# Moving the small steps of LayerNorm's reciprocal root from VectorE to GpSimd in a four-layer attention kernel, with new scheduling limits

## The chip, the cores and the metric

The kernel runs on one core of a Trainium2 chip. The core has a matrix engine (TensorE, PE in the profile; PEld are its weight loads), a vector engine (VectorE, DVE), an engine for activation functions (ScalarE, ACT), a general engine (GpSimd, POOL) and one that here only issues transfers (SyncE, SP). Each executes its own instructions in order and waits for the others by semaphores. The metric is device time of one execution in microseconds; less is better.

## The reference

The input is 2048 tokens of 512 features in bf16. Four residual layers follow each other, of two kinds, A, B, A, B. Each takes the LayerNorm of the running sum (mean and variance over the 512 features, no scale or shift):

```python
def _layernorm(x, axis=-1, eps=1e-05):
    m = jnp.mean(x, axis=axis, keepdims=True)
    v = jnp.var(x, axis=axis, keepdims=True)
    return (x - m) / jnp.sqrt(v + eps)
```

Both kinds have 32 heads of 16 features. Layer B is full softmax attention over all 2048 tokens. Layer A works on four segments of 512 tokens: causal softmax attention inside a segment, mixed by a gate per head with a linear attention over a memory `M`, `z` that the segments before have filled through `phi(t) = where(t > 0, t + 1, exp(t))`. Both end in a projection with 512 x 512 weights, which is added to the running sum.

## The kernel before

A `Builder` writes the program out ahead of time. All instructions pass through a recorder (`Sched.add`), which keeps an order for each engine, derives the semaphore waits from buffers read and written, and keeps a running estimate of when each engine will be free. The builder's choices hang on this estimate and on limits; the dictionary `PLAN` gives limits for each stretch of 40 units, and `set_limits` (called in `attention`) puts them in force.

The main loop, `attention`, goes by units. A unit (`unit`) makes scores of two or three banks, each 128 keys by 512 queries of one head, on TensorE, and one ScalarE instruction turns them into exponentials, 128 x 1024 or 128 x 1536 (L1691, tile `pT`). The weighted sums with the values, whose 17th column counts the denominators, follow two units later. There are 1549 units. In a unit with two banks for ScalarE one or two more banks can go to VectorE, which makes exponentials out of integers: a first affine step reads the scores from PSUM (L1213), then two shifted copies of 1024 or 2048 columns follow (L1267, L1284), and TensorE adds the three.  Their tiles lie in `dxt` or in the spare room of `KA`, `QA`, `VA`, `wA` and `wB`. In layer A the causal mask is added by a matmul with `tri` or set by GpSimd on the exponentials (L1705). GpSimd also makes most masked copies of queries (L1581, `qm`) and multiplies in the division by the denominators (L1838, `ob`), where `POOL_DIV` is 1.

All else is background work, generators that yield what they need next and how much of TensorE and VectorE it takes: `task_A` and `task_B` (LayerNorm, transposes, projections of one segment), `task_mem`, `task_out`. After each unit `background` runs as much of it as the credits allow. PSUM copies go to VectorE, or to ScalarE where the estimate has VectorE later by `EVAC_ACT` (`evac`, L603 and L605). `keep_busy` and `fill_gap` (L560) put matmuls with zeros into holes of TensorE.

LayerNorm of a segment is `ln_part`: statistics of four tiles of 128 tokens on VectorE (L714, L716), then the reciprocal root of four variances for each of 128 tokens, on a tile `lnw` of 128 x 4. For the first segment ScalarE computes it (L722). For the 15 others eight small VectorE steps do it: the variance plus epsilon (L727), a first guess by integer arithmetic on the bits (L729), and two Newton steps of three instructions (L732 to L734). Then `normalize` (L743) writes the normalized tile `xn`, on VectorE, or on GpSimd in stretches with `POOL_XN=1`, and a transposing DMA (L612, on SP) brings it into `xT` for the projections. `xn` has two buffers, so the third tile waits for the first one's transfer.

Of the kernel before, what the change touches and what calls it, by code (L numbers as in the profile page):

```python
# [7 lines left out]
ALU = mybir.AluOpType  # L8
# [9 lines left out]
LN_EPS = 1e-5  # L18
# [310 lines left out]
class Builder:  # L329
# [3 lines left out]
        1: dict(ACT1=400, R_LATE=1200, DX_BANK=700, NEAR=18, FILL_DVE=400, BACK=3, CR_W=1900, CR_B=1800, R_PAIRS=2, PAIRS=24, DIV_LATE=800, DVE_LATE=800),  # L333
        2: dict(MARGIN=500, DX_BANK=900, NEAR=8, SLACK=550, EARLY=300, FILL=0.42, CR_B=1200, PART=3, NEARW=20, PAIRS=60, BUSY_WAIT=500, DX_FIN=3000, POOL_QM=1, POOL_XN=1),
        3: dict(ACT1=600, NEAR=8, TAKEN_A=1, SLACK=550, PV_SKIP=900, FILL_DVE=200, BACK=8, CR_W=1900, NEARW=20, OPART=2, TAKEN=0.4, LOW=14, DVE_LATE=800, QWAIT=8, HOLD_AT=40, PHI_LATE=0),
        4: dict(R_LATE=1200, NEARW=40, PAIRS=24, MASK_PE=800, LEVEL=3, TAKEN=0.5, LOW=30),
        5: dict(R_LATE=1500, DX_LATE=900, REST=12, NEAR=8, TAKEN_A=1, R_NEAR=50, PV_SKIP=500, FILL_DVE=400, BUSY_ROOM=900, CR_W=1300, DX_LAG=1, LOW=20, HOLD_SEGS=2),
        6: dict(ACT1=600, NEAR=10, PV_SKIP=200, DX_LAG=3, MASK_PE=800, LEVEL=3, DIV_LATE=2500, BG_BANK=100, QUAD=0),
        7: dict(ACT1=400, REST=16, NEAR=3, SLACK=350, R_NEAR=10, EARLY=0, FILL_DVE=200, BUSY_ROOM=300, CR_B=1800, R_PAIRS=2, PAIRS=999, TAKEN=0.3, QWAIT=8, QMIN=3, HOLD_AT=12, LN1_AT=6),
# [9 lines left out]
        17: dict(MARGIN=800, NEAR=5, SLACK=350, R_NEAR=10, PART=3, OPART=3, PAIRS=60, DIV_LATE=2500, TAKEN=0.4, DVE_LATE=800),
        18: dict(DX_LATE=900, DX_BANK=700, REST=20, PV_SKIP=100, BUSY_ROOM=900, FILL=0.57, CR_A=1700, PART=3, R_PAIRS=2, OPART=4, MASK_PE=800, DVE_LATE=800, BG_BANK=100, QUAD=0, QWAIT=3, QMIN=4),  # L350
        19: dict(MARGIN=600, R_LATE=1200, DX_LATE=900, PV_SKIP=500, FILL_DVE=100, BACK=6, CR_B=1200, R_PAIRS=2, MASK_PE=800, DIV_LATE=2500, BUSY_WAIT=500, QWAIT=3, QMIN=4),
        20: dict(MARGIN=600, DX_LATE=900, EVAC_ACT=300, SLACK=550, PV_SKIP=100, CR_B=1200, R_PAIRS=2, MASK_PE=800, DIV_LATE=2500, BUSY_WAIT=500, GAP=1, BG_BANK=100, QWAIT=3, QMIN=3, HOLD_AT=40, LN1_AT=6, BUSY_BACK=800),
        21: dict(FILL_DVE=200, BACK=10, FILL=0.53, CR_W=1300, CR_B=1800, CR_A=1700, CARRY_W=0, NEARW=20, LEVEL=3, BG_BANK=400, QMIN=1, HOLD_MAX=0),
        22: dict(ACT1=200, DX_LATE=500, NEAR=10, PV_SKIP=200, EARLY=500, FILL=0.53, CR_B=1800, CARRY_W=1500, OPART=2, DX_LAG=1, MASK_PE=800, LEVEL=3, DIV_LATE=800, DVE_LATE=800, BG_BANK=100, QUAD=0, LN1_AT=6),
        23: dict(R_LATE=1200, R_NEAR=50, FILL_DVE=200, BACK=8, CR_A=1200, NEARW=40, OPART=4, PAIRS=999, LEVEL=3, TAKEN=0.25, QUAD=0, QMIN=4, HOLD_SEGS=2),
        24: dict(R_LATE=1500, DX_LATE=900, EVAC_ACT=100, REST=12, NEAR=8, TAKEN_A=1, SLACK=250, R_NEAR=50, PV_SKIP=100, EARLY=500, FILL_DVE=200, CR_W=1300, CR_A=1200, DX_LAG=1, LOW=20, BG_BANK=100, POOL_QM=1),
        25: dict(ACT1=300, MARGIN=600, R_LATE=2200, EVAC_ACT=1500, NEAR=18, CR_W=1900, CR_B=1800, R_PAIRS=2, DX_LAG=1, PAIRS=999, DIV_LATE=800, TAKEN=0.5, DVE_LATE=800, BG_BANK=400, PHI_LATE=300),
        26: dict(MARGIN=500, DX_LATE=700, REST=10, SLACK=350, EARLY=500, FILL_DVE=200, BUSY_ROOM=300, BACK=8, CR_W=1500, R_PAIRS=2, PAIRS=24, DIV_LATE=800, TAKEN=0.3, BG_BANK=100, QWAIT=8, QMIN=4, LN1_AT=6),
        27: dict(MARGIN=800, DX_BANK=700, REST=4, NEAR=10, SLACK=350, EARLY=500, FILL_DVE=200, BUSY_ROOM=300, BACK=8, CR_W=1500, PART=1, R_PAIRS=2, PAIRS=24, TAKEN=0.3, BG_BANK=100, QWAIT=8, QMIN=4, LN1_AT=6),
        28: dict(EVAC_ACT=800, NEAR=5, SLACK=350, R_NEAR=10, BACK=6, CARRY_W=400, NEARW=40, OPART=3, PAIRS=60, DIV_LATE=2500, BUSY_WAIT=0, TAKEN=0.3, DVE_LATE=800, BUSY_BACK=800),  # L360
        29: dict(DX_BANK=900, SLACK=700, PV_SKIP=100, EARLY=100, FILL_DVE=200, BUSY_ROOM=300, BACK=10, FILL=0.47, CR_W=1500, PART=3, R_PAIRS=2, TAKEN=0.3, DVE_LATE=800, LN1_AT=3, BUSY_BACK=800),
        30: dict(ACT1=300, MARGIN=800, REST=12, SLACK=700, PV_SKIP=100, EARLY=100, BACK=6, FILL=0.42, CR_W=1500, CARRY_W=400, PART=3, R_PAIRS=2, MASK_PE=800, DIV_LATE=2500, DVE_LATE=800, QWAIT=3, HOLD_MAX=0),
        31: dict(DX_LATE=700, DX_BANK=700, REST=20, PV_SKIP=100, BUSY_ROOM=900, FILL=0.57, CR_A=1700, PART=3, R_PAIRS=2, OPART=4, DX_LAG=3, MASK_PE=800, BUSY_WAIT=500, TAKEN=0.3, DVE_LATE=800, BG_BANK=100, QMIN=4, DX_FIN=3000),
        32: dict(MARGIN=400, NEAR=12, PV_SKIP=100, FILL_DVE=100, BUSY_ROOM=300, FILL=0.55, CR_W=1500, CARRY_W=400, R_PAIRS=2, OPART=3, GAP=3, DVE_LATE=800, QWAIT=8, QMIN=1, HOLD_AT=40, POOL_QM=1),
# [3 lines left out]
        36: dict(ACT1=300, DX_LATE=900, DX_BANK=700, REST=20, NEAR=3, PV_SKIP=900, BUSY_ROOM=900, FILL=0.57, CR_B=1800, CR_A=1700, PART=3, R_PAIRS=2, NEARW=90, OPART=3, DX_LAG=1, MASK_PE=200, LOW=20, DVE_LATE=800, QWAIT=3, QMIN=4),
        37: dict(MARGIN=400, NEAR=12, PV_SKIP=100, FILL_DVE=100, BUSY_ROOM=300, FILL=0.55, CR_W=1500, CARRY_W=400, R_PAIRS=2, OPART=3, GAP=3, DVE_LATE=800, QMIN=1, HOLD_AT=40, POOL_QM=1),
        38: dict(DX_LATE=700, REST=8, SLACK=250, R_NEAR=20, CR_W=1300, R_PAIRS=2, NEARW=90, PAIRS=999, LEVEL=1, LOW=20, GAP=1, DVE_LATE=800, BG_BANK=400, QUAD=0),  # L370
# [3 lines left out]
    MASK_PE = 500  # L374
# [1718 lines left out]
```

## Time and profile before

| | |
|---|---|
| median of 3 runs | 1736.19 us (1736.08 to 1737.96) |
| profiled execution | 1740.29 us |
| its span, first to last instruction | 1738.5 us |
| granted TensorE clock, mean | 0.996 |
| instructions | 46910 |

The profile's page gives each engine's busy time and share of the span, then the chain of work that ended last, by engine and by line, then groups of instructions: line, engine, operation, tile written and tiles read, shapes and count, then busy time in us and mean duration in ns, then the idle time of the engine just before them with what ended it. Busy time of a group is a union: where instructions overlap, it is less than count times mean. A list of one tile's or line's instructions gives minimum, median and maximum in ns. A table by windows gives each engine's busy time and instruction count, the granted clock, the share of DMA and GB/s. In the timeline the first two columns are the start and the duration in us. A list of waits gives total time in us, how often, and the longest.

### The profile page before, as it was taken

Reading aid. Unit: us, or ns where it says so; the run is one execution under the profiler, and the core shown is the slowest. Engines: PE = TensorE matmul, PEld = TensorE weight load, DVE = VectorE, ACT = ScalarE, POOL = GpSimd, SP = SyncE. Lnnn points to the kernel's source line nnn. Section 1 sums busy time; section 2 is a strip of 40 time slices with the busy share of each in tenths; the row PEclk is TensorE's granted clock in tenths of the full one; section 3 lists DMA queues with packets and bytes.
Section 4 is the critical chain, followed back from the end, with each engine's and each line's share of the span. In section 5 each row is a group of like instructions: output and inputs, shape, how many; then the busy total and the mean of one; then the engine's idle time right before and its main releaser. Section 6 shows DMA issues by size and latency. Waiting matters only on the chain.

```text
span 1738.5 us, 46910 instructions
## 1 busy us (share of the span) xinstructions
PE 1623.1 (93%) x19531; PEld 577.5 (33%) x19531; DVE 1521.2 (88%) x2928; ACT 1700.7 (98%) x1595; POOL 211.8 (12%) x321
## 2 busy tenths in 40 slices
PE   8999899999999999999999999999999999999999
PEld 5553434322222523522225222432222222222226
DVE  6757576999998689899996999889999999999997
ACT  8899999999999999999999999999999999999998
POOL 3211301110200402100003010110011000000000
PEclk9999999999999999999999999999999999999999
DMA  6210211000202131102111211011011000000000
GB/s 177 38 20 19 38 20 26 14 14 7 35 20 59 32 93 32 33 10 56 47 22 30 47 41 44 8 31 39 8 26 38 10 14 14 19 11 17 16 14 18
DMA packets 148438, 54.56 MB, mean 31 GB/s; under 512 B 128768, under 2 KB 147712, under 8 KB 148224
## 3 DMA queue, kind: packets, MB, share of 16 engines
q1 hardware_dynamic: 148224, 51.56, 13.8%
q8 instruction: 153, 2.51, 0.6%
q14 instruction: 61, 0.50, 0.1%
HBM read 18.88 MB, written 2.10 MB: 12 GB/s over the span
## 4 chain that ended last, share of the span: by engine, by line
ACT 48%; PE 31%; issue 13%; DVE 7%; SPq 0%; POOL 0%; DMA 0%; ACTq 0%; DVEq 0%
ACT pT L1691 47%; PE ps L545 31%; DVE KA L1213 1%; DVE dxt L1213 1%; ACT amem L810 1%; DVE lnst L714 1%; SPq L612 0%; DVE wA L1213 0%; PE ps L560 0%; POOL xn L743 0%; DVE VA L605 0%; DVE qm L1581 0%; DVE dxt L1267 0%; DVE dxt L1284 0%; DVE VB L605 0%
## 5 line engine op out<-in xcount | busy, mean ns | idle before, releaser
L1691 ACT ACTIVATE pT<-ps 128x1024 bf16<-128x1024 f32 (+1 forms) x1549 | 1668.6, 1246 | 24.4 <-PE ps L545 19.8
L545 PE MATMUL ps<-qm,KB 32*128 32x512 bf16 x4096 | 559.7, 385 | 79.5 <-ACT pT L1691 64.3
L545 PE MATMUL ps<-pT,VB 128*17 128x512 bf16 x2909 | 494.7, 384 | 2.1 <-DVE KA L1213 0.5
L545 PEld LDWEIGHTS ps<-qm,KB 32*128 32x128 bf16 x4096 | 145.0, 91 | 606.5 <-ACT pT L1691 518.3
L1213 DVE TENSOR_SCALAR KA<-ps 128x512 uint16<-128x512 f32 (+1 forms) x413 | 295.2, 724 | 13.0 <-PE ps L545 8.7
L1213 DVE TENSOR_SCALAR dxt<-ps 128x512 uint16<-128x512 f32 (+1 forms) x325 | 232.6, 721 | 16.5 <-PE ps L545 13.3
L545 PE MATMUL ps<-dxt,VB 128*17 128x512 bf16 x993 | 217.6, 381 | 0.0
L545 PEld LDWEIGHTS ps<-pT,VB 128*17 128x17 bf16 x2909 | 115.6, 87 | 285.7 <-issue 271.3
L1838 POOL TENSOR_TENSOR ob<-tb,rd 128x512 bf16<-128x512 bf16 x31 | 33.9, 1092 | 801.9 <-DVE rd L1834 801.9
L1213 DVE TENSOR_SCALAR wA<-ps 128x512 uint16<-128x512 f32 (+1 forms) x169 | 120.8, 723 | 2.6 <-PE ps L545 1.2
L545 PE MATMUL ps<-QA,VB 128*17 128x512 bf16 x420 | 118.3, 384 | 0.0
L1705 POOL TENSOR_SCALAR_AFFINE_SELECT pT<-pT 128x256 bf16<-128x256 bf16 (+4 forms) x128 | 67.6, 541 | 413.8 <-ACT pT L1691 413.8
L545 PE MATMUL ps<-woB,zero 128*32 128x512 bf16 (+1 forms) x353 | 117.5, 382 | 0.1
L545 PE MATMUL ps<-VA,VB 128*17 128x512 bf16 x420 | 114.1, 382 | 0.0
L545 PE MATMUL ps<-wA,VB 128*17 128x512 bf16 x534 | 113.1, 381 | 0.0
L545 PE MATMUL ps<-qm,KA 32*128 32x128 bf16 (+2 forms) x1536 | 93.6, 256 | 17.8 <-ACT pT L1691 12.8
L1581 POOL TENSOR_SCALAR qm<-QB,par 128x512 bf16<-128x512 bf16 x98 | 79.5, 821 | 234.8 <-PE ps L545 215.8
L545 PE MATMUL ps<-VA,pT 128*128 128x51 bf16 (+1 forms) x2540 | 103.9, 187 | 2.1 <-POOL pT L1705 0.9
L545 PE MATMUL ps<-KA,VB 128*17 128x512 bf16 x420 | 101.0, 383 | 0.0
L545 PEld LDWEIGHTS ps<-VA,pT 128*128 128x128 bf16 x2540 | 89.6, 96 | 20.9 <-issue 7.3
L1267 DVE TENSOR_SCALAR dxt<-dxt 128x1024 uint16<-128x1024 uint16 (+1 forms) x216 | 85.7, 420 | 1.2
L1213 DVE TENSOR_SCALAR wB<-ps 128x512 uint16<-128x512 f32 (+1 forms) x108 | 84.6, 792 | 1.6 <-PE ps L545 1.0
(167 smaller groups left out, 1946.6 us busy)
## 6 DMA issues: line engine op xcount, KB each, us to landing
wB<-in_B_wqkv_dram SPq DMA_DIRECT2D x48, 128.0 KB, 2.3
wA<-in_A_wk_dram SPq DMA_DIRECT2D x16, 128.0 KB, 2.2
wA<-in_A_wq_dram SPq DMA_DIRECT2D x16, 128.0 KB, 2.3
wA<-in_A_wv_dram SPq DMA_DIRECT2D x16, 128.0 KB, 2.4
out_dram<-x SPq DMA_DIRECT2D x8, 256.0 KB, 2.2
x<-in_A_x_dram SPq DMA_DIRECT2D x3, 512.0 KB, 9.5
wB<-in_B_wqkv_dram SPq DMA_DIRECT2D x1, 1536.0 KB, 11.8
oT<-ob SPq DMA_TRANSPOSE x63, 2.4
```

The costliest lines, as they stand in the source:

```text
L545: self.sc.add("pe", lambda e: e.matmul(out, lhsT, rhs, start=start, stop=stop, skip_group_check=True), reads=reads, banks=[(bank, "w", all ...
L714: self.op("dve", (lambda i, t: lambda e: e.bn_stats(st[:, k, i, 0:6], self.x[:, t, :]))(i, t), reads=[self.b_x[t]], writes=[bs], ns=690, p ...
L810: self.op("act", lambda e: e.activation(et, src, ACT.Exp), reads=bsrc, writes=self.b_amem, ns=1023, gap=915)
L1213: self.op("dve", lambda e: e.tensor_scalar(d, o, SCALE * LOG2E * 128, 127.0 * 128 + EXP_BIAS, op0=ALU.mult, op1=ALU.add), writes=[self.b_d ...
L1267: self.op("dve", (lambda d, s, c: lambda e: e.tensor_scalar(d, s, float(c), None, op0=ALU.add))(d, s, c), reads=[self.b_dxt[b][0]], writes ...
L1581: self.op(eng, (lambda m, q, col: lambda e: e.tensor_scalar(m, q, col, 0.0, op0=ALU.mult, op1=ALU.add))(m, q, col), reads=[bq, self.b_par] ...
L1691: self.sc.add("act", (lambda dst, src: lambda e: e.activation(dst, src, ACT.Exp, scale=SCALE))(dst, src), writes=self.b_pT[slot * 3 + i:sl ...
L1705: self.op("pool", (lambda blk, pat: lambda e: e.affine_select(blk, blk, pattern=pat, compare_op=ALU.is_ge, fill=0.0, base=0, channel_multi ...
L1838: self.op(eng, lambda e: e.tensor_tensor(ob, t[:, :, :, 0:16], rb, ALU.mult), reads=[br] + self.b_tb, writes=self.b_ob[oi], **(dict(ns=125 ...
```

## The change

GpSimd adds epsilon to the variances and does both Newton steps; VectorE keeps the integer first guess between them. A Newton step `y * (1.5 - 0.5 * v * y * y)` was three instructions, two of them with a scalar and two tensors; it now is four, three plain products and one affine step `-0.5 * t + 1.5`. So nine instructions on GpSimd and one on VectorE take the place of eight on VectorE, for each of 15 segments. In the recorder such a step has `ns=125, gap=110`, and the background work no longer reserves 560 ns of VectorE's credit for a Newton step.

All stretches of `PLAN` but the first and the last get other limits; among them four with `POOL_DIV=0` (10, 15, 16, 25; none before), and `POOL_XN=1` in stretches 2, 13, 22 and 24 (2 and 13 before). With them the whole order after the first units is another one.

```diff
@@ Builder.PLAN
...
-        22: dict(ACT1=200, DX_LATE=500, NEAR=10, PV_SKIP=200, EARLY=500, FILL=0.53, CR_B=1800, CARRY_W=1500, OPART=2, DX_LAG=1, MASK_PE=800, LEVEL=3, DIV_LATE=800, DVE_LATE=800, BG_BANK=100, QUAD=0, LN1_AT=6),
+        22: dict(ACT1=200, DX_LATE=900, NEAR=10, PV_SKIP=200, EARLY=500, BACK=3, FILL=0.53, CR_B=1800, CARRY_W=1500, OPART=2, DX_LAG=1, MASK_PE=800, LEVEL=3, DIV_LATE=800, GAP=1, DVE_LATE=800, BG_BANK=100, QUAD=0, LN1_AT=6, POOL_XN=1),
...
-        24: dict(R_LATE=1500, DX_LATE=900, EVAC_ACT=100, REST=12, NEAR=8, TAKEN_A=1, SLACK=250, R_NEAR=50, PV_SKIP=100, EARLY=500, FILL_DVE=200, CR_W=1300, CR_A=1200, DX_LAG=1, LOW=20, BG_BANK=100, POOL_QM=1),
+        24: dict(R_LATE=1500, DX_LATE=900, EVAC_ACT=100, REST=12, NEAR=8, TAKEN_A=1, SLACK=250, R_NEAR=50, PV_SKIP=100, EARLY=500, FILL_DVE=200, CR_W=1300, CR_A=1200, CARRY_W=1500, DX_LAG=1, LOW=20, POOL_QM=1, POOL_XN=1),
...
+    POOL_LN = 1
...
@@ Builder.ln_part
-        self.op("dve", lambda e: e.tensor_scalar(v, var, LN_EPS, None, op0=ALU.add), reads=self.b_lnst[k], writes=[bw], ns=165)
+        root = "pool" if self.POOL_LN else "dve"
+        step = lambda fn, reads: self.op(root, fn, reads=reads, writes=[bw], **(dict(ns=125, gap=110) if self.POOL_LN else dict(ns=165)))
+        step(lambda e: e.tensor_scalar(v, var, LN_EPS, None, op0=ALU.add), self.b_lnst[k])
         vi, yi = v.bitcast(dt.int32), y.bitcast(dt.int32)
         self.op("dve", lambda e: e.tensor_scalar(yi, vi, -0.5, RSQRT_MAGIC, op0=ALU.mult, op1=ALU.add), reads=[bw], writes=[bw], ns=165)
         for it in range(2):
-            yield [], 0, 560
-            self.op("dve", lambda e: e.scalar_tensor_tensor(tt, y, -0.5, y, op0=ALU.mult, op1=ALU.mult), reads=[bw], writes=[bw], ns=165)
-            self.op("dve", lambda e: e.tensor_tensor(tt, tt, v, ALU.mult), reads=[bw], writes=[bw], ns=165)
-            self.op("dve", lambda e: e.scalar_tensor_tensor(y, tt, 1.5, y, op0=ALU.add, op1=ALU.mult), reads=[bw], writes=[bw], ns=165)
+            yield [], 0, 560 * (not self.POOL_LN)
+            step(lambda e: e.tensor_tensor(tt, y, y, ALU.mult), [bw])
+            step(lambda e: e.tensor_tensor(tt, tt, v, ALU.mult), [bw])
+            step(lambda e: e.tensor_scalar(tt, tt, -0.5, 1.5, op0=ALU.mult, op1=ALU.add), [bw])
+            step(lambda e: e.tensor_tensor(y, tt, y, ALU.mult), [bw])
         return k
```

More of the change, by code (lines that the diff above doesn't have):

```diff
@@ L336 @@
[L336 to L339, printed above, removed]
@@ L349 @@
[L349 to L352, printed above, removed]
@@ L368 @@
[L368 to L370 removed]
+        1: dict(ACT1=400, R_LATE=1200, DX_BANK=700, NEAR=18, TAKEN_A=1, FILL_DVE=400, BACK=3, CR_W=1900, CR_B=1800, R_PAIRS=2, NEARW=20, PAIRS=24, MASK_PE=800, DIV_LATE=800, DVE_LATE=800),
@@ new lines @@
+        2: dict(MARGIN=500, DX_BANK=900, NEAR=8, SLACK=550, EARLY=300, FILL=0.42, CR_B=1200, PART=3, NEARW=20, PAIRS=60, BUSY_WAIT=500, LOW=30, QMIN=1, PHI_LATE=300, DX_FIN=3000, POOL_QM=1, POOL_XN=1),
+        3: dict(ACT1=600, REST=4, NEAR=8, TAKEN_A=2, SLACK=550, PV_SKIP=900, FILL_DVE=200, BACK=8, CR_W=1900, NEARW=20, OPART=2, TAKEN=0.4, LOW=14, DVE_LATE=800, QWAIT=8, HOLD_AT=40, PHI_LATE=0),
+        4: dict(R_LATE=1200, DX_LATE=700, EVAC_ACT=1500, FILL=0.4, R_PAIRS=0, NEARW=40, PAIRS=24, MASK_PE=800, LEVEL=3, TAKEN=0.5, LOW=30),
@@ new lines @@
+        5: dict(R_LATE=1500, DX_LATE=900, REST=12, NEAR=8, TAKEN_A=1, R_NEAR=50, PV_SKIP=500, FILL_DVE=400, BUSY_ROOM=900, FILL=0.47, CR_W=1300, PART=1, DX_LAG=1, LOW=20, HOLD_SEGS=2),
+        6: dict(ACT1=600, NEAR=10, PV_SKIP=200, CARRY_W=0, DX_LAG=3, MASK_PE=800, LEVEL=3, DIV_LATE=2500, BG_BANK=100, QUAD=0),
+        7: dict(ACT1=400, REST=16, NEAR=3, SLACK=350, R_NEAR=10, EARLY=0, FILL_DVE=200, BUSY_ROOM=300, CR_B=1800, PART=1, R_PAIRS=2, OPART=2, PAIRS=999, TAKEN=0.3, QWAIT=8, QMIN=3, HOLD_AT=12, LN1_AT=6),
@@ new lines @@
+        8: dict(MARGIN=800, NEAR=10, BACK=2, CR_W=1300, NEARW=40, DX_LAG=1, DIV_LATE=2500, BUSY_WAIT=0, DVE_LATE=800, QWAIT=3, QMIN=3, HOLD_MAX=0, PHI_LATE=300),
+        9: dict(ACT1=400, DX_BANK=700, NEAR=18, SLACK=350, FILL_DVE=400, BACK=3, CR_W=1900, CR_B=1800, R_PAIRS=2, PAIRS=24, DIV_LATE=800, DVE_LATE=800),
+        10: dict(R_LATE=1000, DX_LATE=500, DX_BANK=700, NEAR=5, TAKEN_A=1, SLACK=350, R_NEAR=50, CARRY_W=0, R_PAIRS=2, PAIRS=999, DIV_LATE=800, BUSY_WAIT=0, TAKEN=0.5, PE_LOW=4, DVE_LATE=1700, BG_BANK=100, QUAD=0, HOLD_MAX=0, PHI_LATE=300, LN1_AT=6, POOL_DIV=0),
@@ new lines @@
+        11: dict(R_LATE=1200, DX_LATE=900, R_NEAR=10, EARLY=0, BUSY_ROOM=900, FILL=0.42, CR_A=1200, OPART=4, MASK_PE=800, DIV_LATE=2500, DVE_LATE=800, BG_BANK=400, QMIN=4, HOLD_SEGS=2, PHI_LATE=0, POOL_QM=1, BUSY_BACK=800),
+        12: dict(ACT1=300, MARGIN=600, R_LATE=2200, EVAC_ACT=1500, NEAR=18, CR_W=1900, CR_B=1800, R_PAIRS=2, DX_LAG=1, PAIRS=999, DIV_LATE=800, TAKEN=0.5, DVE_LATE=800, BG_BANK=400, PHI_LATE=300, DX_FIN=3000),
+        13: dict(MARGIN=350, R_LATE=1500, DX_LATE=900, TAKEN_A=1, EARLY=300, BUSY_ROOM=300, CARRY_W=1500, PART=3, OPART=3, PAIRS=999, MASK_PE=800, BUSY_WAIT=0, GAP=3, QUAD=0, QWAIT=3, HOLD_SEGS=2, POOL_XN=1),
@@ new lines @@
+        14: dict(ACT1=200, DX_LATE=500, PV_SKIP=200, CARRY_W=0, DX_LAG=3, LEVEL=3, DIV_LATE=2500, BG_BANK=100, QUAD=0),
+        15: dict(ACT1=400, MARGIN=400, R_LATE=2200, EVAC_ACT=300, DX_BANK=700, REST=8, TAKEN_A=2, PV_SKIP=500, EARLY=300, FILL_DVE=400, BUSY_ROOM=400, BACK=4, CR_W=2200, CR_A=1700, CARRY_W=400, PART=1, DX_LAG=3, DIV_LATE=800, DVE_LATE=800, BG_BANK=100, POOL_DIV=0),
+        16: dict(ACT1=200, DX_LATE=500, PV_SKIP=200, DX_LAG=3, MASK_PE=800, LEVEL=3, DIV_LATE=2500, BG_BANK=400, QUAD=0, POOL_DIV=0),
@@ new lines @@
+        17: dict(MARGIN=800, NEAR=5, SLACK=350, R_NEAR=10, BACK=3, PART=3, OPART=3, PAIRS=60, DIV_LATE=2500, TAKEN=0.4, BG_BANK=100, POOL_QM=1),
+        18: dict(ACT1=200, DX_LATE=500, NEAR=10, PV_SKIP=200, EARLY=500, FILL=0.53, CR_B=1800, OPART=2, DX_LAG=1, MASK_PE=800, LEVEL=3, DIV_LATE=800, DVE_LATE=800, BG_BANK=100, QUAD=0, LN1_AT=6),
+        19: dict(MARGIN=600, R_LATE=1200, DX_LATE=900, TAKEN_A=1, PV_SKIP=500, FILL_DVE=100, BACK=6, CR_B=1200, R_PAIRS=0, DX_LAG=3, MASK_PE=800, DIV_LATE=2500, BUSY_WAIT=500, QMIN=4),
@@ L371 @@
+        38: dict(DX_LATE=700, REST=20, SLACK=250, R_NEAR=20, CR_W=1300, R_PAIRS=2, PAIRS=999, LEVEL=1, LOW=20, GAP=1, DVE_LATE=800, BG_BANK=400, QUAD=0),
         39: dict(R_LATE=2200, CR_W=1900, R_PAIRS=2, PAIRS=24, DIV_LATE=800),
```

41 lines of the change are left out of this document (16 added, 25 removed).

## The prediction

> **What bounds the kernel now.** I read the page's busy table and its chain first, then the busy time by eighths of the span, then ScalarE's groups and waits, and last the LayerNorm steps themselves.
>
> ```profile
> span 1738.5 us, 46910 instructions
> PE 1623.1 (93%) x19531; PEld 577.5 (33%) x19531; DVE 1521.2 (88%) x2928; ACT 1700.7 (98%) x1595; POOL 211.8 (12%) x321
> ACT 48%; PE 31%; issue 13%; DVE 7%; SPq 0%; POOL 0%; DMA 0%; ACTq 0%; DVEq 0%
> ```
>
> ScalarE (ACT) is busy for 98% of the span and carries the largest part of the chain that ended last. VectorE (DVE) has 7% of that chain and GpSimd (POOL) nothing that the table shows. So the first question about any edit is what it does to the number of columns that ScalarE must turn into exponentials, and the second whether it opens or closes one of the few holes in ScalarE's row. Where those holes are, the eighths tell:
>
> ```profile
> 0.00:217.00 217.00, 195.03 (x2724) 97.99 (x2724) 140.34 (x342) 194.72 (x160) 51.04 (x96) 0.98 0.25 59
> 217.00:434.00 217.00, 203.72 (x2507) 73.11 (x2504) 179.68 (x362) 215.21 (x191) 23.56 (x40) 1.00 0.09 16
> ...
> 868.00:1085.00 217.00, 203.14 (x2357) 69.35 (x2358) 193.84 (x395) 215.12 (x201) 25.62 (x43) 1.00 0.17 37
> 1085.00:1302.00 217.00, 206.77 (x2509) 71.02 (x2501) 201.74 (x384) 215.76 (x208) 25.18 (x38) 1.00 0.10 22
> 1302.00:1519.00 217.00, 203.64 (x2025) 53.66 (x2025) 213.56 (x337) 215.30 (x223) 18.11 (x19) 0.99 0.09 20
> ```
>
> The columns are PE, weight loads, DVE, ACT, POOL, the granted clock and DMA. In the first eighth ACT stands idle for 217 - 194.72 = 22.3 us; in each row after it for 1.2 to 1.9 us (217 - 215.76, 217 - 215.12). DVE has 76.7 us to spare in the first eighth, 23.2 us in that from 868, and 3.4 us in that from 1302. What ends ACT's waits:
>
> ```profile
> ACT pT L1691 <- PE ps L545: 19.8, 46, 2.0
> ACT pT L1691 <- POOL pT L1705: 1.2, 2, 0.6
> ```
>
> Nearly all of it is a score tile that TensorE had not finished, 46 times, 19.8 us. No wait of ACT names a LayerNorm step.
>
> **The change, part by part. First, ScalarE's work.** The instruction order of the two programs can be counted. The exponentials over 1024 columns go from 1015 to 1005, those over 1536 from 534 to 539; PSUM copies on ACT go from 9 to 12 (KA from 2 to 6, QA from 4 to 2, VA from 3 to 4); all else on ACT stays.
>
> ```profile
> L1691 ACT ACTIVATE pT<-ps 128x1024 bf16<-128x1024 f32 x1015 | 977.3, 1108 | 3.9 <-PE ps L545 2.6
> L1691 ACT ACTIVATE pT<-ps 128x1536 bf16<-128x1536 f32 x534 | 764.2, 1509 | 20.4 <-PE ps L545 17.2 <-POOL pT L1705 1.2
> L603 ACT ACTIVATE QA<-ps 128x512 bf16<-128x512 f32 x4 | 2.5, 612 | 0.0
> ```
>
> Instructions overlap, so the price of one is busy time over count: 977.3/1015 = 0.963 us and 764.2/534 = 1.431 us. Ten fewer of the first and five more of the second are -9.6 + 7.2 = -2.5 us. The three extra copies at 2.5/4 = 0.6 us are +1.8 us. Together -0.7 us, all of it on the engine that bounds. If the copies fall into holes of ACT it is -2.5 us; if the exponentials' saving falls into holes it is +1.8 us; as ACT is 98% busy I take -0.7.
>
> **Second, the root itself.** In the kernel before, each of 15 segments runs eight small steps on DVE; one of them as the timeline shows it, and the groups:
>
> ```profile
> 175.94 0.17 DVE L727 TENSOR_SCALAR lnw<-lnst 128x4 f32<-128x4 f32 x1
> ...
> 177.33 0.16 DVE L734 SCALAR_TENSOR_TENSOR lnw<-lnw 128x4 f32<-128x4 f32 x1
> ```
> ```profile
> L743 DVE TENSOR_SCALAR xn<-x,lnst,lnw x52: 399/406/708, 21.9 to 1176.9; 128x512 bf16<-128x512 bf16 x52
> ...
> L727 DVE TENSOR_SCALAR lnw<-lnst x15: 157/161/1153, 17.6 to 1169.4; 128x4 f32<-128x4 f32 x15
> ...
> L743 POOL TENSOR_SCALAR xn<-x,lnst,lnw x8: 2069/2076/2620, 177.6 to 662.9; 128x512 bf16<-128x512 bf16 x8
> ```
>
> From the first start to the last are 1.39 us for seven steps, so a step takes 0.20 us of DVE, of which 0.16 is the instruction and 0.04 the turn to the next. Seven of eight leave DVE (the integer step of the first guess stays): 15 x 7 x 0.20 = 21 us. On POOL they become nine, 135 instructions. No row shows an arithmetic step of 128x4 on POOL. The nearest are its setting and its masking of 128x8:
>
> ```profile
> L658 POOL TENSOR_SCALAR_AFFINE_SELECT hmask<-hmask 128x8 f32<-128x8 f32 x1 | 0.2, 195 | 0.1
> ...
> L657 POOL MEMSET hmask<- 128x8 f32 x1 | 0.1, 106 | 0.0
> ```
>
> With DVE's turn of 0.04 that bounds a step by 0.14 and 0.23 us; it both reads and writes, which is nearer to the masking, so I take 0.2. The eight steps behind the first guess then last 1.6 us (1.1 to 1.9), as long as DVE's whole root did.
>
> They are off DVE but not out of its way. By the written order of the changed program, in 9 of the 15 segments the very next DVE instruction behind the first guess is the normalization L743, which needs the last POOL step; DVE executes in order, so it stands there for the whole POOL chain. (In one more segment 30 other instructions lie in between; in five the normalization itself begins on POOL.) That is 9 x 1.6 = 14 us (10 to 17), and each first guess waits for POOL's shift of the variance, 15 x 0.2 = 3 us. Of the 21 us that leave, some 17 come back as standing. What is late next in such a place are the PSUM copies and the DVE exponentials queued behind L743, and for them TensorE; the cover is DVE's spare time of 23.2 to 76.7 us per eighth where the segments lie (L727 runs from 17.6 to 1169.4). If that cover were gone, all 17 us would press on the scores' banks.
>
> On POOL the shift waits for DVE's statistics, and the Newton steps for DVE's first guess; queued behind them are the masks L1705 and the query copies L1581. In the listing the next of them belongs to exponentials 2 to 32 further on, and POOL is 12% busy, so I cost that at nothing.
>
> **Third, what the new limits move.** By count: ten normalizations go from DVE to POOL, four divisions L1838 come back to DVE, DVE's PSUM reads L1213 become 27 fewer of 512 and 16 more of 1024 columns, and its shifted copies become 64 more of 1024, 34 fewer of 2048 and 18 more of 512 columns. DMA issues stay at 353.
>
> ```profile
> L1213 DVE TENSOR_SCALAR KA<-ps 128x512 uint16<-128x512 f32 x382 | 258.5, 683 | 11.6 <-PE ps L545 7.5 <-DVE wA L1267 0.3
> L1267 DVE TENSOR_SCALAR dxt<-dxt 128x1024 uint16<-128x1024 uint16 x200 | 81.4, 430 | 1.2
> L1284 DVE TENSOR_SCALAR dxt<-dxt 128x2048 uint16<-128x2048 uint16 x70 | 48.2, 702 | 0.3
> L1213 DVE TENSOR_SCALAR KA<-ps 128x1024 uint16<-128x1024 f32 x31 | 37.8, 1219 | 1.3 <-PE ps L545 1.2
> L1042 DVE SCALAR_TENSOR_TENSOR oT<-oT,gfm,phq 128x512 bf16<-128x512 bf16 x24 | 17.9, 751 | 0.5 <-DMA phq<-amem 0.5
> ```
>
> The normalizations: -10 x 0.41 = -4.1 us. The divisions, by the nearest two-tensor step of DVE of that size (0.75): +3.0 us. The reads: -27 x 0.683 + 16 x 1.219 = +1.1 us. The copies: +64 x 0.43 - 34 x 0.70 + 18 x 0.43 (an upper end for 512 columns) = +11.5 us. With -21 + 17 from the root, DVE's occupied time changes by about +7 us on 1521: it is as full as before. At DVE's 7% of the chain, 7 us make +0.5 us; at the eighths' spare time they make nothing. All of it on the path would be +7. I take 0. The normalizations on POOL cost 2.08 us each and so 1.67 us more of delay; by the planner's own count the ten added ones have 125 or more score banks of ready work in front of them, so also 0.
>
> **Fourth, the holes.** The first eighth holds most of them and its order hardly moves: the roots stand at exponentials 1, 29, 37, 106, 110 and 170 before, and at 1, 29, 37, 106, 110 and 171 after; the normalizations come up to three exponentials earlier. TensorE's fill-ins for holes between matmuls go from 242 to 238. So I leave the holes as they are: 0. The ends are that the six middle eighths lose their 1.2 to 1.9 us each (about -9 us) and the rival on the other side below.
>
> **The port.** One row bears on 100 more POOL instructions beside DVE:
>
> ```profile
> 653.88 1.06 POOL L1838 TENSOR_TENSOR ob<-tb,rd 128x512 bf16<-128x512 bf16 x1 [47.82 <-DVE rd L1834]
> ...
> 660.16 2.08 POOL L743 TENSOR_SCALAR xn<-x,lnst,lnw 128x512 bf16<-128x512 bf16 x1 [0.41 <-DMA xT<-xn]
> ```
> ```profile
> 654.25 0.96 DVE L1267 TENSOR_SCALAR VA<-KA 128x1024 uint16<-128x1024 uint16 x1
> ...
> 661.32 0.43 DVE L1267 TENSOR_SCALAR dxt<-dxt 128x1024 uint16<-128x1024 uint16 x1
> ```
>
> A copy on DVE that met POOL's two-tensor step took 0.96 us in place of 0.43, and ended 0.27 us after it. A copy that lay wholly inside POOL's normalization took its plain 0.43 us. So two-tensor steps hold DVE up and the slow normalization does not. Ninety of the 135 new steps are of the first kind, but short: in the five segments whose normalization begins on POOL DVE runs on beside them, 5 x 6 x 0.2 = 6 us at most, in the others DVE stands anyway. The Trainium skill, page "SBUF — State Buffer", section "SBUF: two separate sides", says that the port pair shared by the two engines is an exclusive lock, held for the whole instruction. By that rule the ten further normalizations would hold DVE for up to 10 x 2.08 us as well; the trace agrees for the division and contradicts it for the normalization.
>
> **Sum.** Against the profiled execution (1740.29 us, span 1738.5): -0.7 + 0 + 0 + 0 gives 1739.6. That execution lies 4.1 us above the median of the runs, 1736.19, so against the median the forecast is 1735.5 us: no change that a measurement of this kernel tells, which I put at 0.2%, or 3.5 us.
>
> **Rivals.** *The new limits close holes.* ACT waits for PE 46 times for 19.8 us, and every stretch's limits but two were set anew, which shifts when PE's background matmuls run. For it speaks that these waits are single events of up to 2.0 us; against it that the counts of PE's work and of its fill-ins are nearly the same, and that the first stretch, where the holes are thickest, keeps its limits. A third of the 19.8 gone gives 1735.5 - 6.6 = 1728.9 us.
>
> *POOL's queue becomes a wait early on.* At exponentials 1, 29 and 37 the variance's shift stands in POOL's queue right behind the masks of that very exponential, so DVE, whose next instruction is the first guess, stands until that exponential and its masks are done, and then through the chain.
>
> ```profile
> PEld ps L545 <- POOL pT L1705: 5.0, 18, 0.7
> ...
> L1705 POOL TENSOR_SCALAR_AFFINE_SELECT pT<-pT 128x384 bf16<-128x384 bf16 x16 | 8.4, 522 | 49.9 <-ACT pT L1691 49.9
> ```
>
> One exponential (1.43), a mask (0.52) and the chain (1.6) are 3.5 us; three such, 10.6 us on DVE. It decides once the delay exceeds the banks of work ready there: 14, 10 and 6, that is 5 to 2 exponentials of 1.43 us, so at the second or third of the places. Two of three exposed give 1735.5 + 7 = 1742.5 us. Against it: DVE's 76.7 us of spare time in that eighth, and masks delay TensorE by just 5.0 us in the whole span.
>
> *A hold by every POOL instruction*: if the ten added normalizations held DVE for all their 2.08 us, as the division does, that is 20.8 us and 6 from the steps, in eighths where DVE has 23.2 us to spare; a third reaching ACT gives 1735.5 + 9 = 1744.5 us. The copy of 0.43 us speaks against it. This is what the rule of the Trainium skill's page "SBUF — State Buffer" would make of the change.
>
> *The change does not take effect on DVE at all*, since it stands for as long as it saves: that is in my sum.
>
> **How the numbers follow.** No change 0.40; holes closed 0.36; POOL's queue 0.18 and the hold 0.06, both slower, 0.24. The range reaches from all holes of the six middle eighths gone (1735.5 - 9, and the copies hidden, -1.8: 1725) to the hold's 1744. The likeliest case alone spans 1732.7 to 1739.7.
>
> **What would show it.** Right: ACT's two groups at x1005 and x539 with the same prices per instruction; POOL's new rows at 0.15 to 0.2 us; DVE idle before L743 ended by POOL lnw, ten or more us in all; ACT idle of some 22 us in the first eighth and 1 to 2 in the others. Wrong: POOL steps much over 0.23 us, ACT waits ended by PE that are a third less or more than 19.8 us, or copies L1267 lengthened inside POOL's rows.

## The result, and the profile after

The changed kernel takes 1748.51 us (1748.17 to 1750.41, 4 runs), the kernel before 1736.13 us beside it (1735.13 to 1737.96). The ratio is 1.0072, with a 95% interval from 1.0055 to 1.0090: 0.7% slower, 12.4 us. The forecast was 1735.5 us and no change, with a range from 1725 to 1744.

The profiled execution after took 1748.56 us and is a typical one. That of before, at 1740.29 us, lies 4.1 us above its median, so the two profiles can show only 8.2 us of the 12.4. From the page after, the span, the busy time and the chain by engine:

```profile
span 1746.7 us, 46856 instructions
PE 1628.8 (93%) x19449; PEld 582.2 (33%) x19523; DVE 1510.6 (86%) x2851; ACT 1702.6 (97%) x1593; POOL 260.1 (15%) x469
ACT 47%; PE 25%; issue 13%; DVE 11%; POOL 2%; DMA 1%; ACTq 0%; DVEq 0%; SPq 0%; POOLq 0%
```

ScalarE is busy for 1702.6 us in place of 1700.7 and so idle for 44.1 in place of 37.8: of 8.2 us, 1.9 are work and 6.3 are holes. VectorE is busy for 11 us less, and yet the chain runs through it for 11% of the span in place of 7%. Where the holes are, by eighths (columns as in the prediction: PE, weight loads, DVE, ACT, POOL, clock, DMA):

```profile
0.00:217.00 217.00, 189.34 (x2713) 97.01 (x2741) 136.82 (x315) 196.19 (x165) 63.74 (x146) 0.99 0.25 59
217.00:434.00 217.00, 203.95 (x2495) 74.27 (x2502) 179.90 (x355) 214.19 (x191) 27.10 (x57) 1.00 0.09 16
...
651.00:868.00 217.00, 206.70 (x2416) 73.80 (x2422) 192.75 (x392) 213.77 (x203) 23.38 (x43) 1.00 0.19 43
868.00:1085.00 217.00, 204.66 (x2369) 70.79 (x2378) 192.70 (x379) 213.35 (x198) 41.43 (x71) 1.00 0.17 36
1085.00:1302.00 217.00, 207.18 (x2526) 72.18 (x2525) 198.21 (x362) 213.48 (x203) 35.22 (x53) 1.00 0.10 22
1302.00:1519.00 217.00, 204.54 (x2027) 54.10 (x2024) 213.10 (x342) 216.45 (x219) 19.27 (x21) 1.00 0.09 20
```

The first eighth has 20.8 us of holes (22.3 before). Most of those in the middle have grown: 2.8 us in the one from 217 (1.8 before), 3.7 in that from 868 (1.9), 3.5 in that from 1085 (1.2); only that from 1302 has shrunk, to 0.6 (1.7). The six middle eighths together have 6.3 us more. Where they have grown it is again TensorE that ScalarE waits for, as the list of waits says, and over the span more often, 54 times in place of 46:

```profile
ACT pT L1695 <- PE ps L546: 24.6, 54, 2.2
```

The first eighth is not as equal as it looks. Three later runs, shown below, keep the order of before through the whole of it, and their profiles have 20.1, 17.9 and 19.4 us of holes there; four that keep the order of after have 21.8 to 23.5. So the 4.1 us by which the profile of before lies above its median are mostly there, and the new order loses some 2 us there as well. The same eighth in the run that moved one limit in stretch 17:

```profile
0.00:217.00 217.00, 194.28 (x2762) 97.31 (x2766) 143.53 (x348) 199.07 (x164) 51.90 (x97) 1.00 0.26 60
```

ScalarE's groups:

```profile
L1695 ACT ACTIVATE pT<-ps 128x1024 bf16<-128x1024 f32 x1005 | 972.2, 1093 | 6.6 <-PE ps L546 3.7 <-ACT pT L1695 0.5
L1695 ACT ACTIVATE pT<-ps 128x1536 bf16<-128x1536 f32 x539 | 772.9, 1500 | 24.2 <-PE ps L546 20.9 <-POOL pT L1709 0.6 <-ACT pT L1695 0.2
```

An instruction costs 972.2/1005 = 0.967 us and 772.9/539 = 1.434 us, 3 to 5 ns more each than before. Instructions that follow without a hole overlap: in ScalarE's timeline further down one exponential over 1536 columns lasts 1.45 us and two in a row 2.77, not 2.90. One that stands before a hole does not, so holes also show as busy time; how much of the 3 to 5 ns that makes, no run tells.

The steps of the root, from the list of the tile `lnw` (durations in ns: minimum, median, maximum) and of VectorE's waits, and one root in the timeline of GpSimd:

```profile
L735 POOL TENSOR_TENSOR lnw<-lnw x30: 198/199/301, 18.0 to 1175.8; 128x4 f32<-128x4 f32 x30
...
L747 POOL TENSOR_SCALAR xn<-x,lnst,lnw x18: 2065/2083/2730, 179.5 to 1184.7; 128x512 bf16<-128x512 bf16 x18
L730 POOL TENSOR_SCALAR lnw<-lnst x15: 222/228/332, 17.5 to 1173.6; 128x4 f32<-128x4 f32 x15
```
```profile
DVE xn L747 <- POOL lnw L738: 20.7, 9, 2.3
...
DVE lnw L732 <- POOL lnw L730: 6.1, 8, 2.1
```
```profile
18.03 0.20 POOL L735 TENSOR_TENSOR lnw<-lnw 128x4 f32<-128x4 f32 x1 [0.29 <-DVE lnw L732]
18.31 0.20 POOL L736 TENSOR_TENSOR lnw<-lnw 128x4 f32<-128x4 f32 x1
...
20.01 0.20 POOL L738 TENSOR_TENSOR lnw<-lnw 128x4 f32<-128x4 f32 x1
```

A step lasts 0.20 us, and eight of them start (20.01 - 18.03)/7 = 0.28 us apart. VectorE stands for 2.3 us at each of nine normalizations and for 6.1 us at the first guesses, 26.8 us in all. That is more than the 21 us it was spared. The obvious suspect is this standing. The experiments say otherwise.

### The profile page after: what moved, and what is told of

It reads as the page before. It is cut to its first block, busy times and chain, and to the rows that moved or that the text cites. A ratio compares the mean times of both kernels' runs of the same rounds, so it can differ in the third digit from the quotient of the medians.

```text
span 1746.7 us, 46856 instructions
## 1 busy us (share of the span) xinstructions
PE 1628.8 (93%) x19449; PEld 582.2 (33%) x19523; DVE 1510.6 (86%) x2851; ACT 1702.6 (97%) x1593; POOL 260.1 (15%) x469
## 4 chain that ended last, share of the span: by engine, by line
ACT 47%; PE 25%; issue 13%; DVE 11%; POOL 2%; DMA 1%; ACTq 0%; DVEq 0%; SPq 0%; POOLq 0%
ACT pT L1695 46%; PE ps L546 25%; DVE KA L1217 2%; DVE dxt L1217 1%; DVE lnst L715 1%; ACT amem L814 1%; DVE wA L1217 1%; DVE dxt L1271 1%; DVE xn L747 1%; DMA phq<-amem 0%; DVE QA L1271 0%; POOL xn L747 0%; DMA tb<-ub 0%; DVE wA L1271 0%; DVE lnst L717 0%
## 5 line engine op out<-in xcount | busy, mean ns | idle before, releaser
L1695 ACT ACTIVATE pT<-ps 128x1024 bf16<-128x1024 f32 (+1 forms) x1544 | 1669.2, 1235 | 30.8 <-PE ps L546 24.6
L546 PE MATMUL ps<-qm,KB 32*128 32x512 bf16 x4096 | 566.3, 384 | 76.1 <-ACT pT L1695 55.2
L1217 DVE TENSOR_SCALAR dxt<-ps 128x512 uint16<-128x512 f32 (+1 forms) x333 | 240.1, 726 | 22.8 <-PE ps L546 19.8
L546 PE MATMUL ps<-dxt,VB 128*17 128x512 bf16 x1026 | 225.1, 381 | 0.0
L546 PE MATMUL ps<-woB,zero 128*32 128x512 bf16 (+1 forms) x395 | 128.4, 381 | 0.1
L546 PE MATMUL ps<-QA,VB 128*17 128x512 bf16 x426 | 125.8, 381 | 0.4 <-DVE QA L1271 0.3
L1709 POOL TENSOR_SCALAR_AFFINE_SELECT pT<-pT 128x256 bf16<-128x256 bf16 (+4 forms) x135 | 71.8, 546 | 329.2 <-ACT pT L1695 328.6
L546 PE MATMUL ps<-VA,VB 128*17 128x512 bf16 x426 | 119.6, 381 | 0.0
L546 PE MATMUL ps<-KA,VB 128*17 128x512 bf16 x426 | 111.4, 381 | 0.0
L546 PE MATMUL ps<-qm,KA 32*128 32x128 bf16 (+2 forms) x1536 | 93.1, 255 | 17.9 <-ACT pT L1695 9.5
L1271 DVE TENSOR_SCALAR dxt<-dxt 128x1024 uint16<-128x1024 uint16 (+1 forms) x266 | 104.0, 416 | 1.3
L1217 DVE TENSOR_SCALAR wB<-ps 128x512 uint16<-128x512 f32 (+1 forms) x102 | 77.8, 768 | 2.5 <-PE ps L546 0.8
```

The lines of the kernel that those rows point to most:

```text
L546: self.sc.add("pe", lambda e: e.matmul(out, lhsT, rhs, start=start, stop=stop, skip_group_check=True), reads=reads, banks=[(bank, "w", all ...
L1217: self.op("dve", lambda e: e.tensor_scalar(d, o, SCALE * LOG2E * 128, 127.0 * 128 + EXP_BIAS, op0=ALU.mult, op1=ALU.add), writes=[self.b_d ...
L1271: self.op("dve", (lambda d, s, c: lambda e: e.tensor_scalar(d, s, float(c), None, op0=ALU.add))(d, s, c), reads=[self.b_dxt[b][0]], writes ...
L1695: self.sc.add("act", (lambda dst, src: lambda e: e.activation(dst, src, ACT.Exp, scale=SCALE))(dst, src), writes=self.b_pT[slot * 3 + i:sl ...
L1709: self.op("pool", (lambda blk, pat: lambda e: e.affine_select(blk, blk, pattern=pat, compare_op=ALU.is_ge, fill=0.0, base=0, channel_multi ...
```

## The experiments

The changed kernel differs in two things: which engine executes the root, and, through limits and estimates, what the builder (the planner from here on) writes: the order of nearly all other instructions, and some of their sizes and engines. All of that is called the order below. Theory *engine*: the root on GpSimd makes VectorE late, and that is the 12.4 us. Theory *order*: the new order is slower by itself. To tell them apart an instruction needs one engine for the planner's estimate and another that it is issued to. A few lines in the recorder do that:

```diff
-        e = op.eng
-        ready = max([d.end + LAG[d.eng] if d.eng != e else d.end + 35 for d in op.deps], default=0.0)
+        e = op.est
+        ready = max([d.end + LAG[d.est] if d.est != e else d.end + 35 for d in op.deps], default=0.0)
```

With `est` the order of all engines' other instructions stays, instruction by instruction, what it was.

### The order of before, the root on GpSimd

```diff
-        self.op("dve", lambda e: e.tensor_scalar(v, var, LN_EPS, ...
+        step = lambda fn, reads, ns=165: self.op("pool", fn, reads=reads, writes=[bw], ns=ns, est="dve")
+        step(lambda e: e.tensor_scalar(v, var, LN_EPS, None, op0=ALU.add), self.b_lnst[k])
...
```

> The kernel before with its whole written order kept, on every engine; only the root's instructions are issued to GpSimd, nine in place of seven on VectorE. Theory 'engine' (GpSimd's chain of 0.30 us steps makes VectorE stand at the first normalization, 26.8 us in the changed kernel): most of the 12.4 us, so 1744 to 1750 us. Theory 'order' (the new limits wrote a worse order; where the root runs matters little): 1735 to 1739 us.

1741.38 us, ratio 1.0022 (1.0013 to 1.0032): 0.2% slower, between the two forecasts, about in the middle. VectorE's waits for the root are

```profile
DVE xn L747 <- POOL lnw L738: 7.7, 4, 2.3
DVE lnw L732 <- POOL lnw L730: 4.3, 7, 1.9
```

That these 12.0 us are what costs is not shown: VectorE's own work is 16.8 us less (1504.4 us busy). In the profile the one new large hole of ScalarE, 2.66 us, ends when TensorE's scores come, and TensorE had waited for a transposing DMA that took 4.90 us, where the median of those transfers is 2.5. In the kernel before, ScalarE waits 0.19 us at that place. Whether the new root made that transfer late stays open. From the chain and ScalarE's timeline of this run, and from the timeline before:

```profile
107.24 4.90 DMA xT<-xn
```
```profile
115.01 1.45 ACT L1695 ACTIVATE pT<-ps 128x1536 bf16<-128x1536 f32 x1 [2.66 <-PE ps L547]
```
```profile
114.84 1.45 ACT L1691 ACTIVATE pT<-ps 128x1536 bf16<-128x1536 f32 x1 [0.19 <-PE ps L545]
```

### The order of after, the root on VectorE

```diff
-        root = "pool" if self.POOL_LN else "dve"
-        step = lambda fn, reads: self.op(root, fn, ...
+        step = lambda fn, reads: self.op("dve", fn, reads=reads, writes=[bw], ns=125, gap=110, est="pool")
...
+            step(lambda e: e.scalar_tensor_tensor(tt, y, -0.5, y, op0=ALU.mult, op1=ALU.mult), [bw])
...
```

> The changed kernel with its whole written order kept, on every engine; only the root's steps are issued to VectorE again, in the eight instructions of before. Theory 'engine': back to 1735 to 1740 us, and VectorE no longer waits for lnw. Theory 'order': 1745 to 1750 us.

1749.76 us, ratio 1.0072 (1.0059 to 1.0084), the changed kernel's own. VectorE no longer waits for the root at all, its 26.8 us of standing are gone, and not a microsecond is won. The steps themselves are back on it, so its busy time is 18.2 us more than after; the run tells what the swap is worth, not what standing alone would cost. ScalarE's waits are what they were. From that run's page, and its list of waits:

```profile
PE 1628.2 (93%) x19449; PEld 581.6 (33%) x19523; DVE 1528.8 (88%) x2956; ACT 1701.9 (97%) x1593; POOL 231.8 (13%) x334
```
```profile
ACT pT L1699 <- PE ps L548: 25.2, 54, 2.1
```

Theory *engine* falls. The 12.4 us belong to the written order, which loses them with the root on either engine.

### The order of after, other normalizations

The planner reckons a normalization on GpSimd at 0.80 us; it takes 2.08. Ten of 18 were added by the new limits. Perhaps the order is bad because it trusts that price. First, the late ones back on VectorE:

```diff
-        self.op(eng, lambda e: e.tensor_scalar(xn, ...
+        self.op("dve" if self.step > 200 else eng, lambda e: e.tensor_scalar(xn, ...), est=eng,
```

> The changed kernel with its written order kept, but the normalizations that stand on GpSimd behind exponential 200 (14 of 18) are issued to VectorE. They take 2.08 us on GpSimd where the planner reckons 0.80. Theory 'normalizations' (the planner's wrong price lets the transposes come late): 1741 to 1745 us. Theories 'engine' and 'order': 1747 to 1750 us, as the changed kernel.

1764.69 us, ratio 1.0158 (1.0144 to 1.0172), 16 us slower than the change and than either forecast. The normalizations now stand on VectorE behind a root that is still on GpSimd, which makes VectorE wait 12 times and 27.5 us in place of 9 times and 20.7. That is 6.8 of the 16 us at most; the rest is not taken apart. ScalarE waits for TensorE 67 times:

```profile
ACT pT L1697 <- PE ps L548: 40.9, 67, 4.7
```

So this run does not answer the question, as it puts in new waits. The next one leaves them on GpSimd and makes them short, by leaving out the subtraction of the mean:

```diff
+        if eng == "pool" and self.step > 200:
+            fn = lambda e: e.tensor_scalar(xn, self.x[:, t, :], rstd, 0.0, op0=ALU.mult, op1=ALU.add)
```

> The changed kernel with its written order kept; the 14 normalizations that stand on GpSimd behind exponential 200 are one-scalar steps, 0.70 us as the query copies in place of 2.08 us. The subtraction of the mean is left out of them, so this is not the reference's output. If the planner's wrong price for them (0.80 us) is what opened the holes behind exponential 480, 1739 to 1744 us. If the order itself holds them, 1746 to 1750 us.

1749.36 us, ratio 1.0073 (1.0060 to 1.0085): nothing, although they now last 0.70 us. The planner's price for these normalizations is wrong, but it is not what loses the time.

### Limits and roots crossed

With the planner free, the limits of before with the new root (the `PLAN` of before in the code of after):

> The changed code with the limits of before: the root on GpSimd, and the planner writes a new order around it from limits that were not searched for it. If the new limits are what costs, 1736 to 1742 us, faster than the change. If any order that was not picked among many costs some 10 us, 1745 to 1752 us, the same as the change or slower.

1772.36 us, ratio 1.0207 (1.0191 to 1.0223), 36 us slower than before. And the new limits with the root of before (the `PLAN` of after in the code of before):

> The code of before, root on VectorE, with the new limits: the planner writes a new order from limits that were searched for the other root. If limits and root fit only each other, as before's limits with the new root did (1772 us): 1758 to 1780 us. If the new limits are bad by themselves and the root does not matter: 1745 to 1752 us.

1779.74 us, ratio 1.0259 (1.0227 to 1.0291), 43 us slower. Neither set of limits is good or bad by itself. Each does better with the root beside which it was written; with the root on GpSimd the new limits are 1772.4 - 1748.5 = 24 us faster than those of before. Not all of these losses are holes. In the first of the two runs ScalarE's work grows by 15 us (1715.7 us busy, with 571 exponentials over 1536 columns in place of 534), in the second by 10.6 (1711.3). The first one's waits for TensorE double:

```profile
ACT pT L1695 <- PE ps L546: 39.6, 70, 3.9
```

### One limit moved in the kernel before

Does it take a new root to lose so much? Here the root stays on VectorE as it was, and one number of the whole table changes:

```diff
-        17: dict(MARGIN=800, NEAR=5, ...
+        17: dict(MARGIN=750, NEAR=5, ...
```

> The kernel before, root on VectorE as it was, with one limit of one stretch moved (MARGIN 800 to 750 in stretch 17), so that the planner writes another order from exponential 695 on. Theory 'any order that was not picked costs': 1742 to 1765 us. Theory 'the new root's instructions are what disturbs the planner': 1734 to 1739 us, as before.

1751.51 us, ratio 1.0087 (1.0074 to 1.0101). The order is another one from exponential 695 on, and the kernel is 15 us slower.

```diff
-        8: dict(NEAR=10, BACK=2, ...
+        8: dict(NEAR=10, BACK=3, ...
```

> As the run beside it, with another limit moved (BACK 2 to 3 in stretch 8), another order from exponential 320 on. Theory 'any order that was not picked costs': 1742 to 1775 us. Theory 'the new root disturbs': 1734 to 1739 us.

1767.17 us, ratio 1.0184 (1.0167 to 1.0202), 31 us slower. ScalarE's waits in the two:

```profile
ACT pT L1691 <- PE ps L545: 25.4, 55, 5.8
```
```profile
ACT pT L1691 <- PE ps L545: 32.8, 48, 7.3
```

The first is nearly the changed kernel's line in number and sum, 54 waits and 24.6 us there, though one wait of 5.8 us is among them. Four orders of four origins were tried against that of before, besides the change itself, and all are slower, by 15 to 43 us. That the limits of before were picked because their order came out so well is argued from this, not shown; shown is that a nearby order is much slower.

### Which engine opens the holes of the new order

From exponential 840 to 1000 the changed kernel takes 184.4 us in place of 177.4. Five more of these units have three banks in place of two, at 0.47 us each, so some 5 us are lost; 3.8 of them are holes (4.9 us in place of 1.1). There part of TensorE's projections was left out, and in another run three quarters of VectorE's reads of scores:

```diff
+            few = 64 if 840 <= self.unit_no < 1000 and not start and not stop else 512
```
```diff
+        few = w // 4 if 840 <= self.unit_no < 1000 else w
```

> The changed kernel with its written order kept; for exponentials 840 to 999 the two middle contraction steps of each projection are 64 columns wide in place of 512, so most of their sum is left out and this is not the reference's output. There the changed kernel loses some 5 us more of ScalarE than before. If TensorE's background matmuls between two score units open those holes: 1742 to 1745 us. If VectorE's late reads of PSUM do: 1747 to 1749 us.

> The changed kernel with its written order kept; for exponentials 840 to 999 VectorE's first reads of scores take a quarter of the columns, so most of those exponentials are left out and this is not the reference's output. If VectorE's late reads hold the banks that TensorE needs there: 1742 to 1745 us. If TensorE's own work opens the holes: 1747 to 1749 us.

1748.58 us, ratio 1.0070 (1.0055 to 1.0085), and 1748.03 us, ratio 1.0071 (1.0054 to 1.0089): neither shows a gain, though the intervals leave room for some 3 us. ScalarE's waits in the window from 1009 to 1195 us are, after, with the short projections and with the short reads:

```profile
ACT pT L1695 <- PE ps L546: 3.7, 9, 1.0
```
```profile
ACT pT L1696 <- PE ps L546: 3.7, 7, 1.0
```
```profile
ACT pT L1696 <- PE ps L546: 2.8, 8, 0.9
```

In the kernel before they are 0.6 us, 3 times, in the window of the same exponentials (1009 to 1187). In the two runs these exponentials stand up to 5 us later, which changes the sums by 0.2 or 0.3 us. Neither shortening closes the holes. The stretch itself is 2.1 and 2.9 us shorter in their profiles, and 1.3 in that of the control, so a small share of either engine is not excluded. The control, the same short projections in the order of before:

> The kernel before with its written order kept and the same projections shortened for exponentials 840 to 999 (their sum mostly left out). It has 1.4 to 1.8 us of holes in each of these stretches: 1733 to 1736 us whichever engine opens them; a gain as large as the changed kernel's would say that the shortening, not the order, makes it.

1735.39 us, ratio 0.9993 (0.9984 to 1.0002), no gain either. Which rule of the planner places these holes stays open; neither the projections nor the reads in that place explain most of them.

### A faster kernel

The chain that ended last has one costly place in the kernel before: a pair of normalizations on GpSimd near 177 us, with transposes behind them.

```profile
177.60 4.14 POOL xn L743 x2
```

Order kept, the four normalizations near there go to VectorE, which has room:

```diff
-        self.op(eng, lambda e: e.tensor_scalar(xn, ...
+        self.op("dve" if self.step < 200 else eng, lambda e: e.tensor_scalar(xn, ...), est=eng,
```

> The kernel before with its written order kept; the four normalizations that stand on GpSimd near exponential 110 (4.14 us for the first two, on the chain that ended last) are issued to VectorE, where one takes 0.41 us. The transposes start some 3 us earlier and ScalarE's holes there (5.1 us in stretch 2) shrink: 1732 to 1735 us if that chain sets them; 1736 us if the SP queue does.

1733.99 us, ratio 0.9982 (0.9973 to 0.9990): 0.2% faster than before, the lowest median of this study. ScalarE's timeline before and in this run, where the holes at 190 and 195 us are gone (1.00 and 1.96 us in this profile of before, 0.67 to 1.20 and 0.43 to 1.61 in three others of the same order):

```profile
191.23 1.06 ACT L810 ACTIVATE amem<-phk 128x1024 bf16<-128x1024 bf16 x1 [1.00 <-DMA phk<-KA]
192.19 2.77 ACT L1691 ACTIVATE pT<-ps 128x1536 bf16<-128x1536 f32 x2
196.92 1.45 ACT L1691 ACTIVATE pT<-ps 128x1536 bf16<-128x1536 f32 x1 [1.96 <-PE ps L545]
```
```profile
188.49 1.12 ACT L812 ACTIVATE amem<-phk 128x1024 bf16<-128x1024 bf16 x1
189.45 4.19 ACT L1693 ACTIVATE pT<-ps 128x1536 bf16<-128x1536 f32 x3
193.48 1.10 ACT L812 ACTIVATE amem<-phk 128x1024 bf16<-128x1024 bf16 x1
```

## Why the prediction was wrong, by its steps

**The step that failed is the fourth, the holes.** It said: the order of the first eighth hardly moves, TensorE's fill-ins go from 242 to 238, "So I leave the holes as they are: 0". About the first eighth that seems to hold (22.3 to 20.8 us), but by luck of the execution: by the other profiles of the two orders it lost some 2 us. And the new order is another one everywhere behind it, and there I inferred equal holes from nearly equal counts. The order of after has nearly the same counts and 6.3 us more idle ScalarE in the two profiles, all of it in the middle. With the new order kept and the root back on VectorE the kernel still takes 1749.76 us, so the term put at 0 is worth the whole 12.4 us or nearly so. My reading of the holes was also narrow at its ends: behind the first eighth they go from 1.0 us (from 434) to 6.2 (from 1519 to the end), not from 1.2 to 1.9. The ends I gave the term were wrong on one side: about -9 us below, and above only the rival of GpSimd's queue, though a re-written order can open holes as well as close them. One moved limit, at almost the same counts (1014 and 536 exponentials in place of 1015 and 534), costs 15 us. With an end of +15 on this term the range would have held the result.

**ScalarE's work**, put at -0.7 us, measured +1.9 us: the counts were right, but the price per instruction rose by 3 to 5 ns, as I read it because it contains a part of the holes.

**The root.** The direction was right: what leaves VectorE comes back as standing. The size was off. I bounded a step by 0.14 and 0.23 us and took 0.2; it is 0.28 us from start to start, because the turn to the next step is 0.08 us on GpSimd where it is 0.04 on VectorE. So the standing is 26.8 us, not 17. That the exchange is worth nothing was right in the new order: undoing it won nothing. In the order of before, with 12.0 us of standing, the exchange cost 0.2%. That VectorE's spare time is the reason was argued; no run takes the standing away without putting the work back.

**VectorE as full as before** was right in sign and half the size: -11 us of busy time, +27 of standing, +16 on 1521, against +7.

**The rivals.** *Holes closed*, at 0.36: the opposite came, with TensorE again at the end of the waits. That new limits shift when TensorE does what, the mechanism it named, fits this, and needed a twin on the slow side; no run names the rule. *GpSimd's queue early on*, at 0.18: its side was right, its cause was not. The first eighth has 22.4 us of holes in the new order with the root back on VectorE too, so what it lost it did not lose to the root on GpSimd. *A hold by every GpSimd instruction*, at 0.06: not borne out as a price. The means of VectorE's shifted copies stay (429 ns, and 430 before), and shortening the normalizations by two thirds won nothing:

```profile
L1271 DVE TENSOR_SCALAR dxt<-dxt 128x1024 uint16<-128x1024 uint16 x238 | 96.7, 429 | 1.2
```

But there is a hold, and the prediction's row missed it by chance of place. Two normalizations after, the first from 1075.42, the second from 1077.47 us, and three copies beside them:

```profile
1075.42 4.13 POOL L747 TENSOR_SCALAR xn<-x,lnst,lnw 128x512 bf16<-128x512 bf16 x2 [1.84 <-DMA xT<-xn]
```
```profile
1075.56 0.89 DVE L1271 TENSOR_SCALAR QA<-KA 128x1024 uint16<-128x1024 uint16 x1
1077.70 0.81 DVE L1271 TENSOR_SCALAR VA<-KA 128x1024 uint16<-128x1024 uint16 x1
1079.04 0.79 DVE L1271 TENSOR_SCALAR QA<-KA 128x1024 uint16<-128x1024 uint16 x1
```

The first two copies begin early in a normalization and end 1.04 us after its start; the third runs past the second one's end and ends 0.28 us behind it. The prediction's copy of 0.43 us began 1.16 us in and ended well before the end, in the free middle. All lengthened instructions beside the 18 normalizations add up to 2.8 us of VectorE after (0.9 beside the 8 before), far from the 2.08 us each of that rival.

## What to carry to other kernels

When a change makes a planner write a new order, the sum over moved instructions is the small term; the price of the order itself has to be bounded from both sides, and for a kernel at 98% of its bounding engine the slow side is likely the wide one: all five other orders tried here were slower. To learn what an engine swap is worth, hold the order fixed and swap only the engine: here the new order lost its 0.7% with the root on either engine, while the swap alone cost nothing in the new order and 0.2% in the old one. And compare several executions of one order before reading a difference of a few microseconds between two profiles. And look for single places on the chain in the existing order before searching all of it again: four instructions moved by hand gained what the new limits did not.

## What the runs showed of the hardware

Dependent steps of 128x4 on GpSimd start 0.28 us apart at 0.20 us each, on VectorE 0.20 us apart at 0.16. A normalization of 128x512 with two scalars per partition takes 2.08 us on GpSimd and 0.41 on VectorE, while a query copy of the same size with one such scalar takes 0.70 us there (0.35 on VectorE); the planner's 0.80 us fits the second form, not the first. In place of 18.2 us of its own work, VectorE's 26.8 us of standing, spread over 1.2 ms, made no difference that the runs can tell (1748.51 and 1749.76 us).

GpSimd's normalization of 2.08 us holds VectorE's copies of 1024 columns in its first and its last part, not in between. Beside normalizations of plain length (2.06 to 2.09 us), over the profiles of all runs, 17 copies that began in its first 0.6 us all ended 1.03 to 1.04 us after its start, 22 that lay between 0.75 and 1.62 us took their plain 0.41 to 0.43 us, and 15 of the 16 that ran past its end ended 0.28 us behind it, after 0.45 to 0.91 us.
